# Wider splits behind the gelu, and a written order for every operation of a fused attention and feed-forward kernel

## The chip, the cores and the metric

The kernel runs on one core of a Trainium2 chip. The metric is the time of one execution on the device in microseconds, lower is better. Engines are named as the profile names them: PE is TensorE, PEld its weight loads, DVE VectorE, ACT ScalarE, POOL GpSimd, SP SyncE, whose queue issues most of the DMAs.

## What is computed

```python
def _attn_ref(q, k, v):                       # q, k, v: 8 x 8 x 576 x 64, f32
    k_p = k.reshape(B, H, Sp, 8, D).mean(axis=3)
    v_p = v.reshape(B, H, Sp, 8, D).mean(axis=3)
    scores = np.matmul(q, k_p.transpose(0, 1, 3, 2)) / np.sqrt(D)
    scores = scores - np.max(scores, axis=-1, keepdims=True)
    attn = np.exp(scores)
    attn = attn / (np.sum(attn, axis=-1, keepdims=True) + 1e-09)
    return np.matmul(attn, v_p)

def _moe_ref(x, w_in, w_out):                 # x: 4608 x 512, w_in: 512 x 2048, w_out: 2048 x 512
    h = x @ w_in
    g = h * (1.0 / (1.0 + np.exp(-1.702 * h)))
    return g @ w_out
```

The result of the attention, with heads side by side, is x of the second function: 8 batches of 576 tokens. Keys and values are means over 8 rows, so each head has 72 of them.

## The kernel before

**Numbers.** Everything is f32 at the borders. Inside, a factor is split into a high part and the remainder, and a product is three matmuls: high by high, high by low, low by high. For the first batches the parts are f32 words with fewer bits, later scaled f16.

**Stages.** The attention runs batch by batch (0 to 7), in two pieces of 256 and 320 queries: scores, exponentials, transposes, a split of the weights into `ah` and `al` (L1287, L1292), and value products `pav` (L1304 to L1307). The feed-forward part works on chunks: chunk c is the first 512 tokens of batch c, chunk 8 (B in the code) holds the 64 left-over tokens of all batches. Chunks 0 and 1 are computed directly (`dense`). From chunk 2 on a scheme with seven products in place of eight is used: `combine` (L1400) forms sums of the quadrants of x and splits them (L1391, L1397), `fold` (L1694) forms sums of the weights once and leaves them in DRAM (`wd`), and each `pair` (L1807) fetches its folded weights (`ws`, L1753) through the SyncE queue. A chunk has eight pairs.

**A pair.** A pair makes four quadrants of 256 columns of h, two TensorE banks `ha` and `hb` long: seven products of six matmuls each (L1833). A quadrant is copied out of `ha` (`keep`, L1848, ScalarE or VectorE), gets a half of `hb` added (`plus`, L1856, VectorE), goes through the gelu (L1872, ScalarE), and is scaled into the high f16 part (`scaled`, L355 on ScalarE, L358 on VectorE). The remainder is either one instruction of VectorE (L1888) or two of GpSimd (L1893 scale, L1894 subtract). After that `outputs` (L2073) multiplies with w_out: eight triples of matmuls of 512 columns a pair (L2090 to L2092). Chunk 8 uses seven products for the outputs too (`sevens`, L2205); the sums of w_out that it needs are made on the way (`make_sums`, L2106, `made`).

**Buffers.** Quadrants lie in `c_slot`s (ten, L1787), their f16 parts in eight `g_slot`s each (L1769). The names `shared` and `gall` in the profile are these places.

**Order.** The program collects tasks, each with an engine, a duration, a due time and perhaps a second engine that could do it. `Plan.order` (L173) walks through time, gives each free engine the ready task that is due first, and lets VectorE take a task of GpSimd or ScalarE that is late. The tasks are emitted in that order, and each engine executes its own in the order of emission. SyncE's queue is in order as well: a DMA that has to wait for its buffer holds up those behind it.

## Time and profile before

| | us |
|---|---|
| median of 3 runs | 954.1 (951.91 to 954.55) |
| the profiled execution | 954.56 |
| its span, first to last instruction | 952.7 |
| TensorE busy, mean granted clock | 867.6, 0.965 |
| VectorE, ScalarE, GpSimd busy | 705.0, 675.7, 549.8 |

A page of the profile gives, after the busy times, the span in 40 slices, the DMA queues, the chain of work that ended last, the costliest groups of instructions and the DMA issues. A group's row has its line, engine, operation, names and shapes, the count, the busy time, the mean duration of one in ns, and the idle time ahead of its instructions with what ended it. Further views are cut from the same trace: busy times by stretch, the chain in a stretch, and instructions in order of time. A clock of 1.00 is TensorE's higher level, 2.4 GHz; 0.50 is the lower.

### The profile page before, as it was taken

To read this page: it belongs to the slowest core of one execution; us is meant where nothing else is said; L and a number is where in the kernel's file an instruction comes from. 1 tells how busy PE (TensorE), PEld (TensorE's weight loads), DVE (VectorE), ACT (ScalarE), POOL (GpSimd) and SP (SyncE) were. 2 spreads that over 40 slices of the span, in tenths; PEclk is the share of its full clock that TensorE was granted. 3 is DMA by queue.
4 is the path that set the end of the run, shared out by engine and by line. 5 is a ranking of instruction groups with operands and counts; after the bars stand their busy time and mean duration, and the time that the engine had idled before them with its cause. 6 is when DMAs were issued, how large, how long until landed. Compare 5 with 4: busy or idle time off the path is not lost.

```text
span 952.7 us, 16696 instructions
## 1 busy us (share of the span) xinstructions
PE 867.6 (91%) x5614; PEld 644.7 (68%) x5614; DVE 705.0 (74%) x1393; ACT 675.7 (71%) x1484; POOL 549.8 (58%) x570
## 2 busy tenths in 40 slices
PE   9688899999965999579999999999999987999997
PEld 8567889788843676347667766676667654667875
DVE  4757887986879879888788877887969553445676
ACT  4899874467777786558777887778787855656674
POOL 2658752687889955255466558546444779641233
PEclk9899999999977999779999999999999998999999
DMA  8953321443423663444357434733352353455441
GB/s 265 390 201 75 75 49 58 126 114 93 134 110 98 180 165 87 136 100 128 101 127 192 118 115 123 206 95 113 108 134 78 93 157 117 143 150 178 138 145 45
DMA packets 151317, 125.36 MB, mean 132 GB/s; under 512 B 86336, under 2 KB 108352, under 8 KB 151232
## 3 DMA queue, kind: packets, MB, share of 16 engines
q1 hardware_dynamic: 146384, 115.52, 41.8%
q10 hardware_dynamic: 4848, 8.78, 2.6%
q8 instruction: 44, 0.72, 0.3%
q14 instruction: 41, 0.34, 0.1%
HBM read 102.76 MB, written 21.50 MB: 130 GB/s over the span
## 4 chain that ended last, share of the span: by engine, by line
PE 62%; ACT 14%; DVE 12%; issue 3%; POOL 3%; DMA 3%; SPq 2%; DVEq 0%; ACTq 0%; POOLq 0%
PE ha L1833 11%; PE hb L1833 8%; PE o L2090 7%; PE o L2092 7%; PE o L2091 7%; PE sps L1064 3%; ACT main L1180 3%; PE h L1591 3%; PE h L1592 2%; PE h L1593 2%; PE o L1633 2%; PE o L1634 2%; PE o L1635 2%; PE o_P L2320 2%; ACT shared L1872 1%
## 5 line engine op out<-in xcount | busy, mean ns | idle before, releaser
L1833 PEld LDWEIGHTS <-ws 128*128 128x128 f16 x2016 | 198.7, 99 | 93.9 <-issue 40.0
L1893 POOL TENSOR_SCALAR shared<-shared,smalls 128x256 f32<-128x256 f32 x107 | 107.5, 1004 | 131.5 <-ACT ghall L355 77.4
L1833 PE MATMUL ha<-x,ws 128*128 128x256 f16 x1008 | 142.1, 279 | 21.5 <-ACT x L1397 6.8
L2090 PE MATMUL o<-t,ghall 128*128 128x512 f16 x392 | 150.0, 383 | 0.2 <-ACT osb L1551 0.2
L2091 PE MATMUL o<-t,ghall 128*128 128x512 f16 x392 | 149.8, 382 | 0.0
L2092 PE MATMUL o<-t,glall 128*128 128x512 f16 x392 | 149.6, 382 | 0.0
L1833 PE MATMUL hb<-x,ws 128*128 128x256 f16 x1008 | 136.2, 276 | 11.4 <-DVE shared L1856 9.8
L1872 ACT ACTIVATE shared<-shared,smalls 128x256 f32<-128x256 f32 x170 | 85.2, 505 | 31.8 <-DVE shared L1856 26.1
L1856 DVE TENSOR_TENSOR shared<-shared,hb 128x256 f32<-128x256 f32 x127 | 52.5, 414 | 48.2 <-PE hb L1833 28.7
L1894 POOL TENSOR_TENSOR glall<-shared,ghall 128x256 f16<-128x256 f32 x107 | 76.0, 710 | 8.9
L1591 PE MATMUL h<-x,w 128*128 128x256 f32 (+1 forms) x192 | 64.0, 333 | 10.0 <-ACT g L1608 4.3
L2092 PEld LDWEIGHTS <-glall 128*128 128x128 f16 x392 | 38.6, 98 | 48.1 <-POOL glall L1894 1.5
L1848 ACT COPY shared<-ha 128x256 f32<-128x256 f32 x113 | 41.4, 366 | 34.1 <-PE ha L1833 32.2
L355 ACT ACTIVATE ghall<-shared,smalls 128x256 f16<-128x256 f32 x122 | 61.8, 507 | 4.4 <-ACT osb L1551 0.4
L1593 PE MATMUL h<-x,w 128*128 128x256 f32 (+1 forms) x192 | 61.1, 318 | 0.0
L1592 PE MATMUL h<-x,w 128*128 128x256 f32 (+1 forms) x192 | 61.1, 318 | 0.0
L1621 POOL TENSOR_TENSOR gl<-g,gh 128x512 fp32r<-128x512 f32 x25 | 34.2, 1366 | 40.1 <-ACT gh L1613 34.3
L2090 PEld LDWEIGHTS <-ghall 128*128 128x128 f16 x392 | 38.6, 99 | 25.3 <-issue 0.8
L1180 ACT COPY main<-sc 32x256 f32<-32x256 f32 (+2 forms) x123 | 54.5, 443 | 1.7
L2091 PEld LDWEIGHTS <-ghall 128*128 128x128 f16 x392 | 38.6, 99 | 24.7 <-issue 0.9
L1064 PE MATMUL sps<-k,qt 128*128 128x144 f32 x320 | 48.5, 295 | 5.0 <-DVE left L358 2.1
L1531 POOL TENSOR_TENSOR w<-raw,w 128x512 fp32r<-128x512 f32 x29 | 38.4, 1330 | 20.5 <-ACT w L1524 20.2
(364 smaller groups left out, 2265.6 us busy)
## 6 DMA issues: line engine op xcount, KB each, us to landing
ws<-wd SPq DMA_DIRECT2D x168, 256.0 KB
out_dram<-osb ACTq DMA_DIRECT2D x32, 256.0 KB
raw<-in_moe_w_in_dram SPq DMA_DIRECT2D x15, 512.0 KB
raw<-in_moe_w_out_dram SPq DMA_DIRECT2D x15, 512.0 KB
kv_False<-in_k_dram SPq DMA_DIRECT2D x28, 256.0 KB
kv_True<-in_v_dram SPq DMA_DIRECT2D x28, 256.0 KB
shared<-wd SPq DMA_DIRECT2D x56, 128.0 KB
qr<-in_q_dram SPq DMA_DIRECT2D x112, 40.0 KB
```

Source lines behind the costliest of these rows:

```text
L1064: nc.tensor.matmul(ps()[:, t * PW : (t + 1) * PW], lhsT=qt()[:, s0 : s0 + P], rhs=m.k2()[:, jj], start=True, stop=True,)
L1180: copy(out=main()[32 * r : 32 * (r + 1), :, cols].rearrange("p j t (k a) -> p t j a k", a=2), in_=sc()[rows, ts, :, 16 * r : 16 * (r + 1)] ...
L1591: nc.tensor.matmul(o, lhsT=w[:, 0, j], rhs=xs[:, 0], start=j == 0, stop=False)
L1592: nc.tensor.matmul(o, lhsT=w[:, 1, j], rhs=xs[:, 0], start=False, stop=False)
L1593: nc.tensor.matmul(o, lhsT=w[:, 0, j], rhs=xs[:, 1], start=False, stop=j == NJ - 1)
L1833: nc.tensor.matmul(o, lhsT=wv()[:, r, jj], rhs=xo(k, jj), start=start and n == 0, stop=n == len(terms) - 1,  skip_group_check=not start,)
L1872: lambda: nc.scalar.activation(out=part(i), in_=src(), func=AF.Gelu_apprx_sigmoid, scale=inner()),
L1893: nc.gpsimd.tensor_scalar(out=part(i), in0=part(i), scalar1=outer(), scalar2=None, op0=ALU.mult)
L1894: nc.gpsimd.tensor_tensor(out=gl(), in0=part(i), in1=gh(), op=ALU.subtract)
L2090: nc.tensor.matmul(o(), lhsT=gh()[:, tok], rhs=wp[:, 0], start=start, stop=False)
L2091: nc.tensor.matmul(o(), lhsT=gh()[:, tok], rhs=wp[:, 1], start=False, stop=False)
L2092: nc.tensor.matmul(o(), lhsT=gl()[:, tok], rhs=wp[:, 0], start=False, stop=stop)
```

## The change

Three things change together. First, in chunks 2 to 7 two quadrants share one place of 512 columns (a `Group`). The quadrants 2 and 3 of a pair form one group; quadrant 1 of a pair and quadrant 0 of the next form another. The scaled copy and the remainder are made for 512 columns at a time, and so is the gelu of the second kind of group. GpSimd's scale is a tensor by tensor product with the scale as a broadcast operand. Second, quadrant 3's gelu reads the bank `ha` itself, without the copy. There are now seven group places and six for each f16 part; chunk 8 has its own places and its old path by single quadrants (`single`). Third, the planner is gone. A table of task numbers, `ORDER`, gives the order of all tasks; a negative number means that the task goes to its second engine. Some VectorE tasks of the attention get GpSimd as such a second engine: the weighting, and the remainders `al` and `at`.

```diff
+ORDER = """
+3 0 2074 2075 2076 2077 2078 2079 2080 2081 2082 2083 2084 11 169 170 171 10 162 163 4 31 164 73 172 165 12 7 -168 32
...
-    def dve(n, emit, reads, writes, rate=1.0, due=None, also=(), port=False):
+    def dve(n, emit, reads, writes, rate=1.0, due=None, also=(), port=False, other=None):
+        if other is not None:
+            other = ("POOL", 0.15 + n * 2.15e-3, other, True)
...
                 dve(
                     npc,
-                    lambda ah=ah, al=al, pt=pt: nc.vector.tensor_tensor(
-                        out=al()[:, :npc], in0=pt()[:, :npc], in1=ah()[:, :npc].bitcast(F32), op=ALU.subtract
-                    ),
+                    lambda low=low: low(nc.vector),
                     [pt, ah],
                     [al],
                     port=b >= WEIGHED,
+                    other=(lambda low=low: low(nc.gpsimd)) if b >= WEIGHED else None,
                 )
...
+            before = open_groups.pop(c) if p else Group(f"{c}_b")
+            mine, after = Group(f"{nm}_a"), Group(f"{nm}_b")
+            open_groups[c] = after
+            places = [(g.part(i), g.whole) for g, i in ((before, 1), (after, 0), (mine, 0), (mine, 1))]
...
+        def split_group(g, i0, n, whole_gelu):
+            if whole_gelu:
+                x = g.part(i0, n)
+                gelu_of(256 * n, x, x, [ref(x)], ref(x), g.whole)
...
+            t = scaled(256 * n, lambda: gh()[:, cols], lambda: x()[:, cols], outer, [x], [gh], sbuf=True)
...
             def rest():
                 nc.vector.scalar_tensor_tensor(
-                    out=gl(), in0=part(i), scalar=outer(), in1=gh(), op0=ALU.mult, op1=ALU.subtract
+                    out=gl()[:, cols], in0=x()[:, cols], scalar=outer(), in1=gh()[:, cols], op0=ALU.mult, op1=ALU.subtract
                 )
 
             def rest_of():
-                nc.gpsimd.tensor_scalar(out=part(i), in0=part(i), scalar1=outer(), scalar2=None, op0=ALU.mult)
-                nc.gpsimd.tensor_tensor(out=gl(), in0=part(i), in1=gh(), op=ALU.subtract)
+                nc.gpsimd.tensor_tensor(
+                    out=x()[:, cols], in0=x()[:, cols], in1=outer().broadcast_to([P, 256 * n]), op=ALU.mult
+                )
+                nc.gpsimd.tensor_tensor(out=gl()[:, cols], in0=x()[:, cols], in1=gh()[:, cols], op=ALU.subtract)
...
-        keep(3, ha)
-        got[1, 0] = gelu(1, 0, 3)
-        got[1, 1] = gelu(1, 1, 2)
+            gelu(2)
+            gelu(3, ha)
+            got[1, 1], got[1, 0] = split_group(mine, 0, 2, False)
...
-    order = plan.order()
...
+    tasks = plan.tasks + made.tasks
     with tc.manual_schedule():
-        for t in order:
+        for n in map(int, ORDER.split()):
+            t = tasks[n if n >= 0 else -n - 1]
+            if n < 0:
+                t.swap()
             t.emit()
```

What the order does to the engines shows in three places. In the rows a name is followed by its chunk or batch, pair and a buffer number.

ScalarE in chunk 5, around the copies out of `ha5_3`, before (`ah`, `xt`, `x` belong to batch 6's attention):

```order
L1848 COPY shared15_3109<-ha5_3_7169 128x256
L1872 ACTIVATE shared15_3109<-shared15_3109,smalls_94 128x256
L1358 COPY xt6_0_7267<-pav6_0_2_7306 128x256
L355 ACTIVATE ghall1_3191<-shared15_3109,smalls_94 128x256
L1346 CAST x6_7265<-pav6_0_3_7333 128x256
L1358 COPY xt6_0_7267<-pav6_0_3_7333 128x256
L1872 ACTIVATE gall_3283<-gall_3283,smalls_94 128x256
L355 ACTIVATE ghall1_3191<-gall_3283,smalls_94 128x256
```

and now:

```order
L1997 COPY slots15_3059<-ha5_3_6919 128x256
L1448 CAST x6_6947<-pav6_0_1_6929 128x256
L437 ACTIVATE ghall_3209<-slots14_3240,smalls_94 128x512
L2017 ACTIVATE slots12_3043<-slots12_3043,smalls_94 128x256
L2017 ACTIVATE slots12_3043<-slots12_3043,smalls_94 128x512
L1448 CAST x6_6947<-pav6_0_2_6990 128x256
L1460 COPY xt6_0_6944<-pav6_0_2_6990 128x256
L437 ACTIVATE ghall_3358<-slots12_3043,smalls_94 128x512
L2017 ACTIVATE slots15_3059<-ha5_3_6919,smalls_94 128x256
```

The copy of the last quadrant is gone, its gelu reads `ha`, and scaled copies are 512 wide.

TensorE in batch 3, behind the last value product of its attention (`pav3_1_3`) and ahead of the rest of pair 0, before:

```order
L1833 LDWEIGHTS ws3_0_1_3996
L1833 MATMUL hb3_0_4238<-x3_4385,ws3_0_1_3996 128x256
L1064 MATMUL sps4_0_2_4447<-k22_1741,qt4_0_2_4396 128x144 x2
L1064 MATMUL sps4_0_3_4450<-k22_1741,qt4_0_3_4435 128x144 x2
L1833 LDWEIGHTS ws3_0_2_4049
L1833 MATMUL ha3_0_4228<-x3_4444,ws3_0_2_4049 128x256
```

and now, at the place where the first products of pair 0 that have their x are through:

```order
L2272 MATMUL o2_256_3245<-t1_15_3759,ghall_3358 128x512
L2273 LDWEIGHTS ghall_3358
L2273 MATMUL o2_256_3245<-t1_15_3759,ghall_3358 128x512
L2274 LDWEIGHTS glall_3368
L2274 MATMUL o2_256_3245<-t1_15_3759,glall_3368 128x512
L778 MATMUL vmax4_4323<-ident_79,smalls_94 128x128
```

Ahead of the last products of pair 0 (`ha3_0`) stood scores of batch 4; now output triples of chunk 2 (`o2`) stand there, which came ahead of the value products before. Between `pav3_1_3` and the first product of pair 1 there are 11 such triples of chunk 2 now; there were two of chunk 3.

GpSimd in chunk 7, where the sums of w_out are made (`made`), before (`shared` and `glall` are the gelu's remainders, `x8` and `xt8` the split for chunk 8):

```order
L2127 TENSOR_TENSOR made1_0_9175<-t1_3_2917,t1_2_2270 128x256
L1893 TENSOR_SCALAR shared15_3109<-shared15_3109,smalls_94 128x256
L1894 TENSOR_TENSOR glall1_3217<-shared15_3109,ghall1_3191 128x256
L1657 TENSOR_TENSOR made1_0_9175<-made1_0_9175 128x256
L2127 TENSOR_TENSOR made1_1_9196<-made1_0_9175,t1_2_2270 128x256
L1391 TENSOR_TENSOR xt8_0_9077<-xt8_1_9048,xt8_0_9077 128x512
L1391 TENSOR_TENSOR xt8_1_9048<-xt8_1_9048 128x512
L1657 TENSOR_TENSOR made1_1_9196<-made1_1_9196 128x256
L2127 TENSOR_TENSOR made1_2_9227<-made1_1_9196,t1_3_2917 128x256
L1391 TENSOR_TENSOR xt8_1_9048<-xt8_1_9048,xt8_0_9077 128x512
L1657 TENSOR_TENSOR made1_2_9227<-made1_2_9227 128x256
L2127 TENSOR_TENSOR made1_3_9253<-t1_2_2270 128x256
```

and now (`slots` are the gelu's places, `at7` and `al7` remainders of the attention):

```order
L1389 TENSOR_TENSOR al7_1_3_8578<-mt7_1_3_8535,ah7_1_3_8557 128x320
L2309 TENSOR_TENSOR made1_0_8629<-t1_3_2743,t1_2_2547 128x256
L2309 TENSOR_TENSOR made0_3_8652<-t1_0_2539 128x256
L1493 TENSOR_TENSOR xt7_0_8104<-xt7_0_8104,xt7_1_8513 128x512
L1493 TENSOR_TENSOR x7_8657<-xt7_1_8513,x7_8657 128x512
L1759 TENSOR_TENSOR made1_0_8629<-made1_0_8629 128x256
L1759 TENSOR_TENSOR made0_3_8652<-made0_3_8652 128x256
L2048 TENSOR_TENSOR slots15_3059<-slots15_3059,smalls_94 128x512
L2051 TENSOR_TENSOR glall_3368<-slots15_3059,ghall_3358 128x512
L2309 TENSOR_TENSOR made1_1_8858<-made1_0_8629,t1_2_2547 128x256
L2048 TENSOR_TENSOR slots12_3043<-slots12_3043,smalls_94 128x256
L2051 TENSOR_TENSOR glall_3233<-slots12_3043,ghall_3209 128x256
```

Where sums stood in nearly every second place there are fewer, and some of the chain has gone to VectorE. In chunk 7 GpSimd has 13 instructions on `made` for 55, VectorE 22 for none.

## Rows read from the trace of the kernel before

**Rows 1.** The page, part 1: busy time of each engine, share, instructions.

```profile
PE 867.6 (91%) x5614; PEld 644.7 (68%) x5614; DVE 705.0 (74%) x1393; ACT 675.7 (71%) x1484; POOL 549.8 (58%) x570
```

**Rows 2.** Busy time by stretch: length, engines (instructions), clock granted, DMA share, GB/s.

```profile
0.00:60.00 60.00, 46.53 (x308) 41.50 (x309) 35.33 (x80) 44.44 (x90) 27.21 (x29) 0.94 0.97 339
...
60.00:265.00 205.00, 195.89 (x1069) 166.89 (x1068) 161.69 (x250) 144.72 (x296) 138.67 (x117) 0.99 0.31 86
...
265.00:308.00 43.00, 24.60 (x120) 16.89 (x118) 37.51 (x49) 31.80 (x73) 38.59 (x32) 0.72 0.30 97
...
387.00:423.00 36.00, 23.74 (x103) 15.06 (x102) 31.09 (x67) 17.48 (x33) 12.96 (x11) 0.70 0.38 96
...
500.00:770.00 270.00, 264.63 (x1812) 183.93 (x1811) 211.65 (x475) 210.86 (x475) 155.34 (x173) 1.00 0.45 124
...
782.00:802.00 20.00, 11.53 (x58) 6.74 (x57) 7.05 (x10) 11.63 (x28) 19.20 (x22) 0.83 0.38 119
...
862.00:953.00 91.00, 80.99 (x682) 66.31 (x679) 60.91 (x128) 56.09 (x129) 24.96 (x33) 0.99 0.41 129
```

**Rows 3.** Chain of waits, 291 to 309 us: start, us, what.

```profile
295.94 1.85 DVE kbd L805
...
300.03 0.67 SPq L583
...
304.82 3.15 DMA ws<-wd
```

**Rows 4.** Chain of waits, 398 to 424 us.

```profile
411.58 3.17 POOL x L1391 x2
...
414.80 1.01 PE ha L1833 x4
```

**Rows 5.** Chain of waits, 770 to 803 us.

```profile
769.93 0.22 PE o L2091
...
775.19 4.29 DMA out_dram<-osb
...
782.12 1.15 POOL x L1391
```

**Rows 6.** Groups by line and shape: names, shapes, count, busy us, mean ns, idle before.

```profile
L1872 ACT ACTIVATE shared<-shared,smalls 128x256 f32<-128x256 f32 x170 | 85.2, 505 | 31.8 <-DVE shared L1856 26.1 <-DVE shared L1848 2.8 <-ACT osb L1551 0.8
...
L355 ACT ACTIVATE ghall<-shared,smalls 128x256 f16<-128x256 f32 x122 | 61.8, 507 | 4.4 <-ACT osb L1551 0.4
...
L355 ACT ACTIVATE t<-shared,smalls 128x512 f32<-128x512 f32 x15 | 10.8, 721 | 3.7 <-POOL shared L1672 2.6 <-DVE shared L1672 0.8
...
L1848 ACT COPY shared<-ha 128x256 f32<-128x256 f32 x113 | 41.4, 366 | 34.1 <-PE ha L1833 32.2 <-ACT osb L1551 0.5 <-PE hb L1833 0.4
...
L1893 POOL TENSOR_SCALAR shared<-shared,smalls 128x256 f32<-128x256 f32 x107 | 107.5, 1004 | 131.5 <-ACT ghall L355 77.4 <-DVE ghall L358 41.4 <-PE ha L1833 10.4
...
L1894 POOL TENSOR_TENSOR glall<-shared,ghall 128x256 f16<-128x256 f32 x107 | 76.0, 710 | 8.9
...
L1621 POOL TENSOR_TENSOR gl<-g,gh 128x512 fp32r<-128x512 f32 x25 | 34.2, 1366 | 40.1 <-ACT gh L1613 34.3 <-issue 3.0 <-DVE gh L1617 1.8
...
L1888 DVE SCALAR_TENSOR_TENSOR glall<-shared,smalls,ghall 128x256 f16<-128x256 f32 x47 | 27.6, 587 | 27.8 <-ACT ghall L355 27.5
...
L1391 DVE TENSOR_TENSOR x<-xt,x 128x512 f16<-128x512 f32 x10 | 11.5, 1154 | 3.6 <-ACT x L1397 3.6
```

**Rows 7.** VectorE in order of time, 409 to 414 us: start, us, instruction.

```profile
409.20 0.41 DVE L1349 TENSOR_TENSOR x<-pav,x 128x256 f16<-128x256 f32 x1
...
409.53 0.68 DVE L1391 TENSOR_TENSOR xt<-xt 128x512 f32<-128x512 f32 x1
...
412.20 1.53 DVE L1391 TENSOR_TENSOR xt<-xt,xt 128x512 f32<-128x512 f32 x1
```

**Rows 8.** Waits of TensorE: us in total, times, longest us.

```profile
PE hb L1833 <- DVE shared L1856: 9.8, 9, 5.8
...
PE ha L1833 <- DVE shared L1848: 5.1, 3, 3.9
```

341 lines of the change are left out of this document (138 added, 203 removed), and 204 rows, old and new, of the table ORDER.

## Prediction

> **What bounds the kernel now.** The page's first part comes first: TensorE is busy 91% of the span, no other engine more than 74% [rows 1]. So I ask in which stretches TensorE isn't busy, and cut the span there at the places where TensorE starts certain products. Of the stretches in [rows 2] the long one from 500 to 770 us (24 pairs of batches 4 to 6) has TensorE at 264.6 of 270 us at full clock, 1812 matmuls, 0.149 us each: nothing there but fewer matmuls could help, and the change removes none. Three short stretches are different: 265 to 308 (batch 2, between its first two pairs and its third), 387 to 423 (batch 3, inside its first pair) and 782 to 802 (batch 7, second pair). TensorE issues 120, 103 and 58 matmuls there; at 0.149 us each that is 17.9, 15.3 and 8.6 us of work in 43, 36 and 20 us, so 25, 21 and 11 us are lost, 57 together. Part of the loss is clock: 0.72, 0.70 and 0.83 granted against 1.00 in the long stretch, that is, the engine fell to its lower level of 1.2 GHz after it had been starved.
>
> What ends last in each comes from the chain of waits. The first ends in a run of VectorE work (at its end a key sum of 1.85 us), after which SyncE, whose queue keeps its order, issues other loads from 300.03 on and behind them, at 304.82, the weights of the third pair, which land 3.15 us later [rows 3]. VectorE is 37.5 of 43 and GpSimd 38.6 of 43 busy: the stretch ends when the folding of the weights and the splitting of batch 2 are done. The second ends on two GpSimd subtractions that finish the split of batch 3, with TensorE going on at 414.80 [rows 4], at the end of a ladder of transposes, casts, subtractions and products through VectorE, ScalarE and TensorE, in which GpSimd is busy 13 of 36 us: latency, not load. The third begins with ScalarE standing 4.3 us behind an output DMA and then runs through GpSimd, busy 19.2 of 20, whose queue mixes the split of batch 8 and the gelu remainders with sums made for batch 8 [rows 2, 5].
>
> **The gelu chain, two quadrants at once.** In batches 2 to 7 and the last pair of batch 8 there are 196 quadrants, each with a gelu of 505 ns and a scaled copy of 507 on ScalarE (37 of the copies on VectorE), and a remainder: 134 on GpSimd in two instructions, 1004 + 710 ns, 62 on VectorE at 587 [rows 6]; the row of the largest group stands for each, with 107 of the 134 and 47 of the 62. After it, 90 splits are 512 wide and 12 are 256 (batch 8 keeps its own path). A 512-wide scaled copy on ScalarE is in the trace, 721 ns [rows 6]: two quadrants cost 0.72 for 1.01. Of gelus 42 are 512 wide, 48 read PSUM and save a copy of 0.37. ScalarE gives back 100 x 0.29 for the 100 wide instructions, some 36 x 0.37 for copies and 27 x 0.5 for scaled copies that go to VectorE, 56 us over the span, and more with what is moved off it below. On GpSimd 41 wide and 8 narrow two-step remainders stand where 134 stood. The scale is now a broadcast operand, a form that the trace lacks; from below it is an ordinary subtraction of 512 columns, 1.37; from above twice the 1004 of the present scale, 2.0. I take 1.37, the same width and number of operands: 41 x 2.74 + 8 x 1.7 = 126 us for 134 x 1.71 = 230. At 2.0 it is 26 us more on an engine that is idle for 400; I cost that at nothing. VectorE makes 49 remainders of 512 columns and 4 of 256. The wide form isn't in the trace; ends 0.68 (a 512 subtraction alone [rows 7]) and 1.15 (one that mostly meets GpSimd [rows 6]), I take 0.75, near the first, since GpSimd is lighter: 37 us for 62 x 0.587 = 36. None of this is on TensorE's path in the long stretch, so by itself it is worth nothing there.
>
> **The moves between engines.** VectorE goes from 1393 instructions to 1597, ScalarE and GpSimd lose some 360 and 190. VectorE has to hold that. Its busy time overstates it: an instruction of 0.41 us is followed 0.33 after its start when they queue [rows 7]. Up to the third pair of batch 2 the order puts 466 instructions on VectorE for 378, 33 of them casts and subtractions of the weights at the start, 18 of the folding. Mostly 512 wide, they cost 88 x 0.55 = 48 us; ends 88 x 0.33 = 29, and 88 x 1.15 = 101 if each collides. VectorE was busy 35.3 + 161.7 + 37.5 = 234.5 of the first 308 us [rows 2], so now 282. In the first 60 us it waits for the first loads and can do about 35; the other 247 from there end at 307 if every instruction keeps its present span, and 31 us earlier (386 instructions, 0.08 overlap each) if they queue back to back. I take 298: **10 us** of the first stretch's 25, and the folding that ScalarE and GpSimd lose there (some 40 us of GpSimd) is why it isn't more.
>
> Between 308 and 500 us VectorE's number of instructions is nearly unchanged (333 for 337). There the written order counts: three of the four remainders of the ladder in batch 3 go to GpSimd, the engine that had 23 us idle, and eleven output triples of batch 2 stand between the last value product of the ladder and the second pair, for two of batch 3 now. They are held back from before the ladder, so they add no work; they keep TensorE fed while the split ends. I give **16 us** of 21, a quarter left because the last subtractions are still a chain. In the third stretch 42 of 55 sum instructions leave GpSimd's queue, about 42 x 0.7 = 29 us, and half of them go to VectorE, 7.0 of 20 us busy. What stays is the output DMA ahead of it, 4.3 us that other TensorE work covers today: **10 us** of 11.
>
> On the other side: in the long stretch VectorE gets 525 instructions for 470, 24 us more on 211.6 of 270 [rows 2], 87%. Additions of the second half bank are all on VectorE and TensorE waits for them; I charge **2 us**. At the end some 20 output triples of batch 7 (13 us, three matmuls of 512 columns at 0.22 each [rows 5]) stand behind the first product of batch 8 that stood ahead of it, which only moves work, and VectorE gets 20 us more on 60.9 of 91: **3 us**. DMA issues are the same 695; many are now one by one in SyncE's order, so that a single load may stand before a weight load; the row for it is the first stretch, where SyncE's other issues cost 304.82 - 300.03 = 4.8 us [rows 3]; the same loads stand ahead of the same weights there, so I leave it as it is.
>
> **The sum.** The profiled execution took 954.56 us, span 952.7, the median is 954.1: no difference to reckon with. 954.6 - 10 - 16 - 10 + 2 + 3 = 923.6, so **924 us**.
>
> **The rivals.** *VectorE becomes the bound* (slower). It has the reductions, 1.85 us for a key sum [rows 3], that stay on it, and the additions that TensorE waits for queue behind them in a fixed order. For it: VectorE is already the releaser of TensorE's largest wait, 9.8 us in nine, longest 5.8, and 5.1 more in three [rows 8]; the written order has been given nothing but more work for it. Against it: today's nine waits in 56 pairs. If each pair meets half a reduction, 0.93 us, the 56 pairs lose 52 us: 924 + 52 = 976. The point from which it decides is 31 / 56 = 0.55 us a pair.
>
> *The port.* When VectorE and GpSimd both work in SBUF, VectorE's subtraction of 512 columns takes 1.15 us, 1.53 in one row, for 0.68 alone [rows 6, 7]. Some 85 more wide instructions with two SBUF inputs go to VectorE, and GpSimd's own get wider; at 0.47 lost each, 40 us, 25 of them ahead of 308 and in the ladders. The gains of the first two stretches go: 924 + 26 = 950, no change that can be measured. The Trainium skill (SBUF — State Buffer, SBUF: two separate sides) says that the shared pair of ports is an exclusive lock, held for the whole instruction, and the loser fully blocks. By that rule the wide GpSimd instructions make each collision longer; the two rows agree, a 512-wide one waits 0.5 to 0.9 us. Against it: GpSimd is 118 us less busy in all, so collisions are fewer.
>
> *All of it.* The order fills the three stretches fully and some of the 9 us that TensorE idles in 60 to 265: 954.6 - 57 - 5 = 893.
>
> That the change isn't made at all is out: the instructions' order shows the wide forms and the moves.
>
> **Chances.** Forecast 52%, all of it 15%, the port 16%, VectorE's bound 17%. 924 is the likeliest. The range leaves out half of the second case and most of the last: 896 to 962; it takes in the upper price of the 88 moved instructions up to 38 of its 53 us (101 - 48). About 0.3% (2.9 us) is what a measurement of this kernel can tell from no change. Faster by more: forecast and all of it, and a third of the port case, 72%; within it half of the port case, 8%; slower 20%.
>
> **What would show it.** Right: a third pair of batch 2 that starts before 302 us, granted clock above 0.85 in all three stretches, GpSimd under 60% around the second pair of batch 7, rounds of batches 4 to 6 still 90 us each. Wrong: VectorE at 95% or more between 60 and 300 us with TensorE waiting for weight splits; waits of TensorE for the additions above 30 us in total; rounds of 93 us or more; wide subtractions on VectorE at over 1 us in the mean.

## The result, and the profile after

The changed kernel takes 942.64 us (median of 4 runs, 940.6 to 944.99) where the kernel before, run beside it, takes 953.28: a ratio of 0.9889 (95% interval 0.9858 to 0.9921). It is faster by 1.1%; 3.2% was forecast. The profiled execution took 940.6 us, span 938.6, mean clock 0.982 for 0.965.

The first part of the page, to hold against [rows 1]:

```profile
PE 863.9 (92%) x5614; PEld 640.5 (68%) x5614; DVE 788.4 (84%) x1597; ACT 541.8 (58%) x1121; POOL 400.6 (43%) x376
```

The work went where the order sends it: VectorE has 83 us more, ScalarE 134 and GpSimd 149 less. TensorE has the same 5614 matmuls. Busy time by stretch (length, then the engines in the page's order with instructions in brackets, clock granted, DMA share, GB/s), to hold against [rows 2]; the stretches are cut at the places of the program that answer to those of before:

```profile
0.00:60.00 60.00, 51.79 (x330) 45.81 (x331) 47.60 (x101) 43.26 (x89) 27.56 (x30) 0.97 1.00 329
60.00:292.00 232.00, 210.41 (x1143) 177.56 (x1141) 211.58 (x356) 137.58 (x276) 136.94 (x113) 0.97 0.30 85
292.00:407.00 115.00, 95.30 (x602) 62.82 (x601) 108.71 (x218) 75.42 (x147) 67.72 (x61) 0.94 0.50 140
...
366.00:408.00 42.00, 38.19 (x220) 23.44 (x219) 40.19 (x88) 29.13 (x60) 25.36 (x23) 0.96 0.31 74
477.00:764.00 287.00, 273.40 (x1831) 185.06 (x1829) 241.90 (x524) 166.76 (x339) 90.50 (x87) 1.00 0.40 116
...
784.90:794.30 9.40, 9.25 (x66) 6.44 (x66) 6.17 (x13) 5.44 (x11) 6.97 (x8) 1.00 0.67 221
837.00:938.60 101.60, 93.58 (x739) 71.73 (x737) 73.06 (x177) 46.90 (x116) 23.91 (x34) 0.99 0.41 130
```

The low clocks of [rows 2], 0.72, 0.70 and 0.83, are gone: the 30 us ahead of batch 2's third pair (266 to 296) have 0.93, the ladder of batch 3 (366 to 408) 0.96, the second pair of batch 7 (784.9 to 794.3) 1.00. But 292 to 407 now has VectorE at 108.7 of 115, and the 24 pairs of batches 4 to 6 (the "rounds"), which took 270 us, take 287.

**Where the time is lost, at equal work.** Stretches cut by time can't be compared when work moves between them. So I give every matmul the start-to-start time that its shape has undisturbed in the trace of before, and add these up in order of execution: 819.8 us in every kernel here. Between two marks of that sum, the elapsed time less the work is lost. In the trace of before the marks 160, 240, 300, 360, 640 and 720 lie at 200.5, 310.4, 372.3, 459.0, 747.6 and 841.8 us. The table has the loss in us, for both kernels and for the runs below (each one profiled execution). Cells that an edit doesn't touch differ by up to 3.6 us from kernel to kernel, so a difference of less than 4 isn't read by itself.

| work | before | after | p2 | n1 | e1 | e2 | e5 | t2 | s1 | s3 | u1 |
|---|---|---|---|---|---|---|---|---|---|---|---|
| 0 to 160 | 40.5 | 30.3 | 37.1 | 30.9 | 30.5 | 30.3 | 34.1 | 29.5 | 31.0 | 29.6 | 30.1 |
| to 240 (folding, end of the first stretch) | 29.9 | 29.8 | 33.7 | 31.2 | 29.9 | 30.6 | 47.1 | 29.5 | 31.1 | 30.4 | 30.9 |
| to 300 (batch 2's pairs) | 1.9 | 19.0 | 8.4 | 18.9 | 27.6 | 20.1 | 19.7 | 19.7 | 16.1 | 19.6 | 19.1 |
| to 360 (batch 3's ladder) | 26.8 | 8.8 | 21.7 | 7.7 | 11.4 | 12.8 | 8.8 | 14.2 | 7.6 | 7.7 | 8.2 |
| to 640 (rounds) | 8.5 | 19.3 | 12.8 | 24.8 | 22.1 | 38.6 | 22.1 | 19.0 | 18.9 | 13.9 | 18.2 |
| to 720 (third stretch) | 14.2 | 2.1 | 9.0 | 4.2 | 1.4 | 1.6 | 1.7 | 1.4 | 1.4 | 1.3 | 0.8 |
| to the end | 11.1 | 9.4 | 9.7 | 9.5 | 9.2 | 9.6 | 9.4 | 9.4 | 9.2 | 9.2 | 7.8 |
| sum | 132.9 | 118.8 | 132.4 | 127.2 | 132.0 | 143.6 | 142.8 | 122.7 | 115.2 | 111.6 | 115.1 |

The change gains 10.2 in the first 160 us of work, 18.0 at the ladder, 12.1 in the third stretch and 1.7 at the end. It gives back 17.1 in the pairs of batch 2 and 10.8 in the rounds: 14.1 us in all, the difference of the two spans. (The medians differ by 10.6; the profiled execution is the shortest of its four. That of s1, in the table, is the longest of its four, 3.9 us above their median.)

What TensorE waited for over the whole run (us in total, times, longest us), to hold against [rows 8]:

```profile
PE hb L1982 <- DVE slots L2005: 10.8, 12, 4.1
PE ha L1982 <- ACT slots L2017: 7.3, 2, 6.1
...
PE ha L1982 <- ACT slots L1997: 6.1, 5, 2.3
PE ha L1982 <- DVE slots L1997: 4.2, 5, 1.4
```

All four are waits for a bank to be read out: 28.4 us. The 6.1 is one wait, in batch 2's pairs. TensorE and, below it, ScalarE in order of time there (start, us, instruction, in brackets the idle time before and its releaser):

```profile
359.11 0.38 PE L2274 MATMUL o<-t,glall 128*128 128x512 f16 x1
365.57 1.44 PE L1982 MATMUL ha<-x,ws 128*128 128x256 f16 x6 [6.08 <-ACT slots L2017]
```

```profile
359.05 0.37 ACT L1460 COPY xt<-pav 128x256 f32<-128x256 f32 x1 [6.79 <-DVE x L1451]
359.43 1.28 ACT L1200 ACT_TABLE_LOAD   x1
360.72 1.64 ACT L1200 ACTIVATE sc<-sc 128x1728 f32<-128x1728 f32 x1
362.38 1.28 ACT L2017 ACT_TABLE_LOAD   x1
363.68 0.72 ACT L2017 ACTIVATE slots<-slots,smalls 128x512 f32<-128x512 f32 x1
364.43 0.72 ACT L437 ACTIVATE ghall<-slots,smalls 128x512 f16<-128x512 f32 x1
365.06 0.46 ACT L2017 ACTIVATE slots<-ha,smalls 128x256 f32<-128x256 f32 x1
```

The gelu that reads `ha` itself frees the bank. In ScalarE's fixed order it stands behind a copy that waits 6.8 us for VectorE, and then behind an exponential with a table load on either side of it.

### The profile page after: what moved, and what is told of

It reads as the page before. It is cut to its first block, busy times and chain, and to the rows that moved or that the text cites. A ratio compares the mean times of both kernels' runs of the same rounds, so it can differ in the third digit from the quotient of the medians.

```text
span 938.6 us, 16098 instructions
## 1 busy us (share of the span) xinstructions
PE 863.9 (92%) x5614; PEld 640.5 (68%) x5614; DVE 788.4 (84%) x1597; ACT 541.8 (58%) x1121; POOL 400.6 (43%) x376
## 4 chain that ended last, share of the span: by engine, by line
PE 43%; DVE 37%; ACT 7%; issue 6%; DMA 3%; SPq 2%; POOL 1%; DVEq 0%; ACTq 0%; POOLq 0%
PE ha L1982 9%; PE hb L1982 7%; PE o L2274 4%; PE o L2272 4%; PE o L2273 4%; DVE main L1271 2%; PE sps L1148 2%; DVE slots L2005 2%; DVE sc L1221 2%; DVE tail L1262 1%; DVE stage L1818 1%; DVE qt L1132 1%; DVE al L1389 1%; DVE sc L1179 1%; DVE nm L1171 1%
## 5 line engine op out<-in xcount | busy, mean ns | idle before, releaser
L1982 PE MATMUL hb<-x,ws 128*128 128x256 f16 x1008 | 132.7, 273 | 11.3 <-DVE slots L2005 10.8
L2274 PE MATMUL o<-t,glall 128*128 128x512 f16 x256 | 97.7, 381 | 0.4 <-DVE glall L2043 0.4
L2272 PE MATMUL o<-t,ghall 128*128 128x512 f16 x256 | 97.9, 383 | 0.0
L2273 PE MATMUL o<-t,ghall 128*128 128x512 f16 x256 | 97.6, 381 | 0.0
L2005 DVE TENSOR_TENSOR slots<-slots,hb 128x256 f32<-128x256 f32 x139 | 56.2, 412 | 33.4 <-PE hb L1982 27.0
L2048 POOL TENSOR_TENSOR slots<-slots,smalls 128x512 f32<-128x512 f32 (+1 forms) x40 | 40.5, 1013 | 96.0 <-ACT ghall L437 49.0
L2017 ACT ACTIVATE slots<-slots,smalls 128x256 f32<-128x256 f32 (+1 forms) x108 | 61.2, 576 | 34.3 <-DVE slots L2005 32.7
L1997 ACT COPY slots<-ha 128x256 f32<-128x256 f32 x97 | 35.7, 368 | 78.3 <-PE ha L1982 76.8
L1389 POOL TENSOR_TENSOR al<-mt,ah 128x320 fp32r<-128x320 f32 (+1 forms) x23 | 18.9, 822 | 84.7 <-ACT ah L1385 49.2
L1148 PEld LDWEIGHTS sps<-k,qt 128*128 128x128 f32 x320 | 44.1, 196 | 11.7 <-issue 5.1
L1271 ACT COPY main<-sc 32x384 f32<-32x384 f32 (+2 forms) x100 | 45.7, 457 | 10.5 <-DVE sc L1221 5.2
L1982 PE MATMUL ha<-x,shared 128*128 128x256 f16 x336 | 45.7, 273 | 3.8 <-ACT slots L1997 3.0
L2272 PE MATMUL o<-t,slots 128*128 128x512 f16 x128 | 48.6, 380 | 0.0
L2273 PE MATMUL o<-t,slots 128*128 128x512 f16 x128 | 48.6, 380 | 0.0
L2274 PE MATMUL o<-t,slots 128*128 128x512 f16 x128 | 48.6, 379 | 0.0
```

Source lines behind the costliest of these rows:

```text
L1148: nc.tensor.matmul(ps()[:, t * PW : (t + 1) * PW], lhsT=qt()[:, s0 : s0 + P], rhs=m.k2()[:, jj], start=True, stop=True,)
L1271: copy(out=main()[32 * r : 32 * (r + 1), :, cols].rearrange("p j t (k a) -> p t j a k", a=2), in_=sc()[rows, ts, :, 16 * r : 16 * (r + 1)] ...
L1982: nc.tensor.matmul(o, lhsT=wv()[:, r, jj], rhs=xo(k, jj), start=start and n == 0, stop=n == len(terms) - 1,  skip_group_check=not start,)
L2005: lambda: nc.vector.tensor_tensor(out=part(i), in0=part(i), in1=hb()[:, half * 256 : half * 256 + 256], op=ALU.add),
L2017: lambda: nc.scalar.activation(out=out(), in_=src(), func=AF.Gelu_apprx_sigmoid, scale=inner()),
L2272: nc.tensor.matmul(o(), lhsT=gh()[:, tok], rhs=wp[:, 0], start=start, stop=False)
```

## Experiments

Unless said otherwise an edit changes `ORDER` alone. A label's first letter tells the kind: `e` puts work back on its engine of before, `p` and `n` separate width from order, `t` and `u` move instructions, `s` shortens some, `b` combines two. The runs of before that stood beside them had medians of 953.3 to 955.0; "against after" compares medians with 942.64.

**Width without the written order.** p1 and p2 have the changed kernel's operations and the planner of before, with 82 us a round as in before, and with 96.

```diff
-        for n in map(int, ORDER.split()):
+        for t in order:
```

> The wide chain without the written order: the changed kernel's tasks (groups of two quadrants, gelu from PSUM, second engines for al, at and the weighting), ordered by the planner of the kernel before, with its round length of 82. Theory A (the prediction's: the wide chain is worth nothing on TensorE's path, the stretches are gained by the written order): 948 to 960 us, the losses of batch 2, 3 and 7 still there. Rival B (relief of ScalarE and GpSimd by the wide chain gives the gain, the order by itself little): 938 to 946 us.

> As the run with the planner and the round length 82, but with the round length 96 that the changed kernel's text has for its due times. Theory A: 948 to 965 us, since the round length only shifts due times; Rival B: 938 to 946 us. If the two runs differ by more than 5 us, the due times alone are worth as much as the whole change.

p1: 965.34 us, ratio 1.0120 (1.0084 to 1.0155). p2: 955.32, 1.0018 (1.0001 to 1.0035). The page of p2, and busy time at its three stretches:

```profile
PE 867.9 (91%) x5614; PEld 643.2 (68%) x5614; DVE 688.4 (72%) x1295; ACT 637.8 (67%) x1339; POOL 504.8 (53%) x474
```

```profile
262.00:305.40 43.40, 23.32 (x112) 16.64 (x111) 38.52 (x50) 32.60 (x70) 38.39 (x32) 0.66 0.33 109
389.50:435.50 46.00, 34.54 (x193) 22.84 (x193) 38.30 (x86) 26.62 (x56) 24.32 (x23) 0.81 0.43 107
786.00:802.60 16.60, 10.52 (x69) 6.34 (x67) 4.55 (x7) 8.61 (x19) 16.09 (x19) 1.00 0.51 153
```

ScalarE and GpSimd are 38 and 45 us less busy than in [rows 1], and the time is that of before: the stretches stand where they stood in [rows 2], with low clocks in the first two. With this planner the wide chain is worth nothing, as the prediction had it. But the round length, which only shifts due times, makes 10.0 us between p1 and p2, as much as the whole change; other settings of it weren't tried.

**The written order without width.** n1 executes each 512-wide gelu, scaled copy and remainder as two of 256 at the same place of the order, with GpSimd's scale as the operation with a per-partition scalar that it was before. The gelu that reads `ha` stays.

```diff
-                lambda: nc.scalar.activation(out=out(), in_=src(), func=AF.Gelu_apprx_sigmoid, scale=inner()),
+                lambda: [
+                    nc.scalar.activation(out=o, in_=i, func=AF.Gelu_apprx_sigmoid, scale=inner())
+                    for o, i in (zip(pieces(out()), pieces(src())) if n > 256 else [(out(), src())])
+                ],
```

> The written order without the wide chain: every 512-wide scaled copy, gelu and remainder behind the gelu made as two of 256 columns at the same place of the order, GpSimd's scale as before the change (one scalar a row). Theory A (the wide chain is worth nothing on TensorE's path): 943 to 948 us. Rival B (the written order leans on the room that the wide chain makes; some 100 instructions more on ScalarE at 0.29 us each, 41 on GpSimd at about 0.6, 53 on VectorE at 0.3): 955 to 975 us, slower than the kernel before.

947.93 us, 0.9931 (0.9905 to 0.9957): 5.3 us slower than after, 5.5 of it in the rounds (24.8 for 19.3). So the order, with the gelu out of `ha`, is worth some 6.8 us, the runs of before beside it having 954.7. The width and the form of the scale, which n1 takes back together, are worth another 5, but only in this order.

**The folding and the weight splits.** e5 takes 58 instructions of the folding (48.2 us of VectorE, 180 to 278 us) back from VectorE to the engines that had them; e6 the 35 casts and subtractions of the weights in the first 180 us (28.2 us).

```diff
-735 730 2557 -2553 -2554 -2550 -678
+735 730 2557 2552 2553 2549 -678
```

```diff
-12 7 -168 32 -169 176
+12 7 167 32 168 176
```

> The changed kernel with the folding that VectorE had been given between 180 and 278 us (39 instructions of GpSimd, 19 of ScalarE, 48.2 us on VectorE, 0.83 us each) put back at the same places. Theory 1 (the load on VectorE ahead of batch 2's third pair costs what the prediction priced at 0.55 us each): relief of VectorE, third pair earlier by 10 us or more, 930 to 938 us. Rival: GpSimd, 58% busy there and slower for these (1.3 to 1.4 us), becomes what the folded weights wait for, as in the kernel before: third pair later by 5 to 15 us, 948 to 958 us.

> The changed kernel with the 35 instructions of the weights' splits that VectorE took in the first 180 us (28.2 us; 22 from ScalarE, 13 from GpSimd) put back. The kernel before lost 10 us more than the changed one in that stretch, which the prediction had not named. If these splits on VectorE are the reason, most of it comes back as a loss: 948 to 953 us. Rival: it is the order of the first loads and tasks; then 941 to 945 us.

e5: 964.33 us, 1.0115 (1.0095 to 1.0135), 21.7 against after, with 17.3 in the second row of the table. Its largest wait of TensorE is a new one, for remainders (`gl`) of the first two chunks that GpSimd does late:

```profile
PE o L1734 <- POOL gl L1720: 15.8, 5, 6.3
```

So the moves of the folding are needed by this order. They gain nothing there over before, where GpSimd had both (29.8 for 29.9). e6: 946.38, 0.9923 (0.9899 to 0.9948), 3.7 against after, and 3.1 in the first row, no more than rows differ by that an edit doesn't touch: the splits explain 3 of the 10.2 us gained there at most. What the other 7 come from wasn't tried.

**The ladder of batch 3.** t2 puts nine of the output triples of batch 2 back ahead of the value products, e4 the ladder's remainders back on VectorE.

```diff
--1048 2996 3005
+2987 2994 3026 3009 3023 2963 2993 2995 3032 2996 3005
```

```diff
-2989 2991 -1036 1036
+2989 2991 1035 1036
```

> The changed kernel with nine of the eleven output triples of batch 2 that stand behind the last value product of batch 3's ladder (5.9 us at 395 to 403 us, complete since 382 to 391) put in front of the ladder's last two value products. Theory (the prediction's: these triples keep TensorE fed while the split ends): the loss around batch 3's first pair grows by 4 to 6 us, 946 to 950 us. Rival: the ladder itself became shorter, and the triples only fill what would else be filled by others: 941 to 944 us.

> The changed kernel with the four remainders `al` and one `at` of batch 3's ladder (5.2 us on GpSimd) put back on VectorE at the same places. By the prediction, which gave 16 us to the ladder for these moves and for the triples held behind it: if the moves matter, VectorE, 96% busy there, ends the ladder 3 to 6 us later, 945 to 949 us. Rival: the triples alone keep TensorE fed and VectorE's remainders (0.7 us against 1.0 on GpSimd) are no later: 941 to 944 us.

t2: 947.64, 0.9925 (0.9904 to 0.9946): 5.0 against after, and 5.4 in the ladder's cell. The split of batch 3 ends 5.9 us later, which is what the nine triples take: behind the value products they fill the ladder, ahead of them they hold it up. What they would be worth further ahead, in batch 2's pairs, t2 doesn't show; no run puts them there. e4, with four `al` and one `at`: 943.16, 0.9893 (0.9872 to 0.9914). GpSimd's share in the ladder is worth nothing that can be measured.

**Copies of the attention.** The change has many copies on VectorE that ScalarE had: of scores into `main` and `tail` and of keys. e1 puts 45 of them between 278 and 408 us back on ScalarE (22.6 us; 19 `main`, 15 `tail`, 11 of keys), e2 113 between 408 and 764 us (41.9 us).

```diff
-839 2795 2823 -862 -2720
+839 2795 2823 861 -2720
```

```diff
-3022 -1173 -1178 -1166 3033
+3022 -1173 -1178 1165 3033
```

> The changed kernel (942.6 us median, profiled span 938.6) with 45 copies, 22.6 us of VectorE's work between 278 and 408 us (19 `main`, 15 `tail`, 11 `k`, all of batch 3's and 4's attention), put back on ScalarE at the same places of the order. Theory: VectorE, 66 of 70 and 40 of 42 us busy there, is what TensorE waits for while it loses 17 us more than before; then 8 to 15 us come back, 928 to 935 us, and VectorE falls below 85% there. Rival: ScalarE's order is the limit (TensorE's longest wait, 6.1 us, is for a gelu behind the exponentials and two table loads); then ScalarE, 24 us longer in 130, makes it 942 to 950.

> The changed kernel with 113 copies, 41.9 us of VectorE's work between 408 and 764 us (59 `main`, 30 `tail`, 15 `k`, 9 `left`), put back on ScalarE at the same places. Theory: the rounds of batches 4 to 6 lose 11 us because VectorE, 84 to 89% busy, delivers additions late in bursts; with 42 us off it at least half comes back, 932 to 937 us. Rival: VectorE's average load has room, and the loss comes from ScalarE's in-order queue and from the order itself; then no gain, and with 50 us more on ScalarE (58% now) 942 to 950.

e1: 951.16 us, 0.9975 (0.9959 to 0.9990), 8.5 against after. e2: 965.85, 1.0131 (1.0113 to 1.0149), 23 against after. Busy time by stretch for 70 us of e1 and the 70 of after that answer to them, then TensorE's largest wait of e1 between 278 and 420 us and of e2 over the run:

```profile
298.00:368.00 70.00, 52.98 (x352) 36.12 (x350) 50.38 (x93) 49.13 (x104) 38.95 (x34) 0.92 0.57 158
```

```profile
296.00:366.00 70.00, 54.39 (x364) 37.18 (x363) 65.47 (x122) 44.46 (x84) 39.08 (x35) 0.92 0.60 171
```

```profile
PE ha L1979 <- ACT slots L1994: 10.9, 2, 8.9
```

```profile
PE ha L1978 <- ACT slots L1993: 19.4, 15, 2.7
```

VectorE falls from 65.5 to 50.4 of 70 and the kernel gets slower: ScalarE is no more than 70% busy, but the added copies stand in its queue ahead of the copies out of `ha` that it also makes, and TensorE waits for those banks. Ahead of the wait of 8.9 us ScalarE, below, waits 6.8 us for VectorE (`sc`), then makes twelve copies of scores (at that place of after it makes two), and only then the one out of `ha`:

```profile
329.28 1.44 PE L1979 MATMUL ha<-x,ws 128*128 128x256 f16 x6 [8.92 <-ACT slots L1994]
```

```profile
324.82 0.50 ACT L1259 COPY tail<-sc 32x64 f32<-32x64 f32 x2 [6.82 <-DVE sc L1218]
...
328.85 0.37 ACT L1994 COPY slots<-ha 128x256 f32<-128x256 f32 x1
```

The Trainium skill (Perfetto Trace Analysis, Optimizing Scalar/DVE Operations) says that if VectorE is saturated it may make sense to offload some work to ScalarE. Here VectorE was busy 108.7 of 115 us from 292 to 407, and taking 22.6 us off it in that way cost 8.5: the measurement decides, for copies that keep the places of an order made for VectorE. An order made for them on ScalarE wasn't tried. What counted was how soon the bank was read, not how full the engine was.

**Which engine holds the time?** In the `s` kernels some instructions are shortened where they stand, so that what follows may start earlier; what they leave out is missing from the result.

```diff
-                    out=red(), in_=raw().rearrange("p i (w d) -> p i d w", w=POOL), axis=AX.X, op=ALU.add
+                    out=red(), in_=raw().rearrange("p i (w d) -> p i d w", w=POOL)[:, :, :, 0:1], axis=AX.X, op=ALU.add
```

```diff
+            m = n if c == B or reads[0] is ha else n // 16
...
-                lambda: nc.scalar.activation(out=out(), in_=src(), func=AF.Gelu_apprx_sigmoid, scale=inner()),
+                lambda: nc.scalar.activation(out=out()[:, 0:m], in_=src()[:, 0:m], func=AF.Gelu_apprx_sigmoid, scale=inner()),
```

```diff
-                    out=x()[:, cols], in0=x()[:, cols], in1=outer().broadcast_to([P, 256 * n]), op=ALU.mult
+                    out=x()[:, cols][:, 0:32], in0=x()[:, cols][:, 0:32], in1=outer().broadcast_to([P, 32]), op=ALU.mult
```

The first is s1 (the two reductions of 1024 columns; VectorE is 37 us less busy), the second s2 (ScalarE 29 less; it also takes another scale factor behind the gelu), both together are s3; the third is s4 (GpSimd 38 less).

> The changed kernel with VectorE relieved and no other engine loaded: the 24 sums over 8 rows of keys and values (1.94 us each) read one row in eight, some 40 us off VectorE, 5 to 6 us a batch (the means are left out of the computation). Theory: VectorE is what TensorE waits for in batches 2 and 3 (94 to 96% busy from 296 to 408 us) and in the rounds; 15 to 30 us come back: 912 to 928 us. Rival: every engine's queue is in a fixed order, TensorE's losses are latency along the chain through ScalarE, and VectorE's load is not the limit: 936 to 943 us.

> The changed kernel with ScalarE relieved and no other engine loaded: the gelus in place of chunks 2 to 7 (the groups of 512 columns and quadrants of 256 that don't read PSUM) work on a sixteenth of their columns, the rest is left out of the computation; some 80 instructions, about 24 us off ScalarE. Theory S (the rest of the loss hangs on ScalarE's in-order queue): 10 us or more come back, 925 to 933 us. Rival (ScalarE at 58% has room): 938 to 943 us.

> The changed kernel with both reliefs: the 24 row sums of VectorE shortened (40 us) and the gelus in place of chunks 2 to 7 shortened (24 us of ScalarE). If the two engines take turns in being late, both together give more than the sum of each: below 920 us. If only VectorE's load counts: 930 to 935 us, as with the short sums alone.

> The changed kernel with GpSimd relieved: the scale ahead of its gelu remainders works on 32 columns instead of 512 or 256 (48 instructions, some 40 us off GpSimd, the rest of the scaling left out of the computation). By the port (VectorE's instructions wait while GpSimd holds the port) and by output triples that wait for remainders: 932 to 938 us. Rival: GpSimd is idle half of the time and nobody waits for it: 940 to 944 us.

Against after, s1 gains 9.6 us (933.08; 0.9780, 0.9741 to 0.9819), s2 4.2 (938.45; 0.9838, 0.9818 to 0.9859), s3 10.0 (932.67; 0.9777, 0.9757 to 0.9797), s4 7.5 (935.11; 0.9813, 0.9779 to 0.9847). No engine is the bound by itself: of 37 us taken off VectorE a quarter comes back, and of 38 off the least busy engine a fifth. By the sign set for it s3 speaks against engines that take turns in being late: it should have come in below 920, and it takes what s1 takes. The loss in the rounds stays for s1 and s2 (18.9, 18.8) and falls to 13.9 in s3, but these are single executions, that of s1 its longest, so a joint effect isn't shown. The page of s4:

```profile
PE 863.0 (92%) x5614; PEld 640.7 (69%) x5614; DVE 776.7 (83%) x1597; ACT 541.9 (58%) x1121; POOL 362.4 (39%) x376
```

VectorE executes the same 1597 instructions, none of them shortened, and is 11.7 us less busy (776.7 for 788.4): its own take longer when GpSimd is busier. That is the port rival's mechanism, and a part of what s4 gains; how much of the 7.5 us it is and how much are triples that get their remainders sooner isn't told apart.

**Waits at the head of a queue.** 392 instructions read a bank out (copies, additions, gelus of `ha`). From the end of the product (for an addition, of the copy that it adds to, where that is later) to their start passes 0.49 us in the mean in before, 0.89 in after; in the rounds 0.36 and 1.00. u1 moves 124 of them forward in their engine's queue, one of them, for instance, by 42 places:

```diff
+3451 3480 1519
...
-3456 -1524 3480 3498
+3456 -1524 3498
```

u2 also moves 64 other ScalarE instructions and 19 output triples. Some of them pass earlier users of the same place, so u2 computes something else, and its time tells of the queues alone.

> The changed kernel with 124 of the 392 copies, additions and gelus that free TensorE's banks moved forward in the order of their own engine (VectorE or ScalarE), each to where its input was complete; together they stood 162 us in the queues behind other work. No engine gets more or less work. Theory Q (the written order puts the instructions that TensorE waits for behind others; VectorE's and ScalarE's load by itself is not the limit): the loss in batch 2's pairs and in the rounds shrinks, 8 to 18 us come back, 925 to 935 us. Rival: what is passed (exponentials, transposes, splits) is on the path as well, and comes late instead: 940 to 950 us.

> On top of the order with the feeders first (937.3 us): on ScalarE 64 gelus, scaled copies and exponentials moved ahead of instructions that stood at the head of its queue waiting (35 us of ScalarE's waits filled, batch 3's exponentials at 353 us among them), and 19 output triples moved into TensorE's remaining stalls. No engine gets more or less work. Theory (waits at the head of in-order queues are the cause, in ScalarE's too): TensorE's stall of 5 us at 360 us shrinks to 1, and 927 to 933 us in all. Rival: the chain through VectorE (its copies that wait for GpSimd's end, its reductions of 1.9 us) sets the pace: 935 to 940 us.

u1: **937.33 us, 0.9832 (0.9803 to 0.9860)**, runs of 936.68 to 937.66, all below every run of after: faster than both kernels, by 16 and 5 us. u2: 937.48, 0.9828 (0.9805 to 0.9851), nothing beyond u1. In u1 the wait falls to 0.50 us in the mean (0.55 in the rounds), but the loss in the rounds only from 19.3 to 18.2. So these waits cost some 5 us over the run, and taking most of them away leaves most of the 10.8 in the rounds; what was passed may come late instead.

**More filler, more GpSimd.** t1 moves 27 output triples within their queues to where TensorE stalls; b2 is t1 with 32 remainders of 408 to 764 us (25.8 us of VectorE) on GpSimd.

```diff
-2909 2965 -965 2970 2898 2971
+2898 2922 2929 2970 2971
```

```diff
--1251 1254 -3100 3132
+-1251 1254 3099 3132
```

> The changed kernel with 27 output triples (0.65 us each, 17.5 us of work) moved forward in TensorE's order, into 17 places between 214 and 724 us where TensorE stood still (28 us together) while those triples, whose operands were complete, stood 1 to 70 tasks behind. No engine gets more or less work. Theory: the losses are TensorE's own fixed order, which waits at its head while ready products stand behind; 8 to 16 us come back, 927 to 935 us. Rival: the stalls are set by the supply from VectorE and ScalarE, and a triple used early is missing later; then 938 to 943 us.

> The changed kernel with the 27 output triples moved into TensorE's stalls (939.7 us alone) and the 32 gelu remainders that VectorE had been given between 408 and 764 us (25.8 us) put back on GpSimd (two instructions, about 2.2 us each). If VectorE's load in the rounds costs 0.25 us for each us, as with the short row sums, and GpSimd (113 of 356 us busy) has the time: 932 to 936 us. Rival: GpSimd's remainders are 1.4 us later each and output triples wait: 940 to 950 us.

t1: 939.71, 0.9845 (0.9827 to 0.9862), 2.9 against after. b2: 947.64, 0.9938 (0.9914 to 0.9962), 7.9 slower than t1, with 26.4 for 17.5 lost in the rounds. GpSimd was busy 92 of 299 us there, and still it is no place for this work: a remainder takes 1.09 + 1.18 us on it for 0.81 on VectorE (rows below). Whether that or the meeting of the two engines costs it isn't told apart.

**The sums for batch 8.** e3 puts 41 of the sums of w_out (`made`) back on GpSimd.

```diff
-2027 4033 1942 -4798 -4018
+2027 4033 1942 4797 -4018
```

> The changed kernel with the 41 sum instructions (`made`, 17.8 us) that VectorE had been given put back, 30 on GpSimd and 11 on ScalarE, at the same places. By the prediction's term for the second pair of batch 7, GpSimd's queue was the limit there and the sums leaving it were worth 10 us: 949 to 955 us, the loss around batch 7's first pairs returning. Rival: with gelu remainders 512 wide GpSimd (30 of 73 us busy there) holds the sums as well, and the gain there came from the wide remainders: 941 to 945 us.

945.76 us, 0.9920 (0.9905 to 0.9935): 3.1 against after, and 4.5 for 2.1 lost in the third stretch. At most some 3 of the 12.1 us gained there are the sums'.

## Why the prediction was off

**The chain and the moves (costed at nothing in the rounds): right in kind.** p2 shows that the wide chain is worth nothing with the planner of before; in the written order width and the form of the scale are worth 5 us (n1). The groups by line and shape (names, shapes, count, busy us, mean ns, idle before), to hold against [rows 6]:

```profile
L2048 POOL TENSOR_TENSOR slots<-slots,smalls 128x512 f32<-128x512 f32 x33 | 36.0, 1092 | 79.7 <-ACT ghall L437 46.1 <-DVE ghall L440 21.5 <-PE sps L1148 6.7
L2017 ACT ACTIVATE slots<-slots,smalls 128x512 f32<-128x512 f32 x36 | 25.8, 719 | 17.5 <-DVE slots L2005 16.9 <-ACT osb L1653 0.4
L2051 POOL TENSOR_TENSOR glall<-slots,ghall 128x512 f16<-128x512 f32 x26 | 30.8, 1183 | 2.0
L2043 DVE SCALAR_TENSOR_TENSOR glall<-slots,smalls,ghall 128x512 f16<-128x512 f32 x27 | 21.8, 809 | 0.5 <-ACT ghall L437 0.4
L2017 ACT ACTIVATE slots<-ha,smalls 128x256 f32<-128x256 f32 x41 | 19.3, 470 | 27.7 <-PE ha L1982 24.7 <-DMA left_dram<-left 1.9 <-ACT osb L1653 0.4
L1262 DVE COPY tail<-sc 32x64 f32<-32x64 f32 x30 | 12.6, 421 | 2.9 <-POOL sc L1221 2.3
L1493 DVE TENSOR_TENSOR x<-xt,x 128x512 f16<-128x512 f32 x14 | 11.0, 785 | 0.8 <-ACT x L1499 0.7
L2048 POOL TENSOR_TENSOR slots<-slots,smalls 128x256 f32<-128x256 f32 x7 | 4.5, 640 | 16.3 <-DVE slots L440 13.4 <-ACT ghall L437 2.9
```

The 0.72 of a wide gelu was right, the 0.75 of VectorE's wide remainder measured 0.81, and the broadcast scale on GpSimd 1.09, below the lower bound of 1.37.

**The first stretch (-10): right in size, wrong in place.** The third pair of batch 2 starts at 295.8 us, where 298 was forecast, with 468 VectorE instructions ahead of it for 466. But the loss up to there had been cut in the first 160 us of work (40.5 to 30.3): VectorE does 47.6 us of its work in the first 60 us, where I gave it some 35 as in [rows 2], and TensorE 51.8 for 46.5. In the stretch itself nothing was gained (29.9 to 29.8). That the start came out so near 298 is luck: the sum took the first 60 us as they were.

**The ladder (-16): the step that failed.** Its cell does fall from 26.8 to 8.8. But the triples had been batch 2's filler: its cell rises from 1.9 to 19.0. Both lie between the last write of batch 2's split and that of batch 3's, an interval that the attention of batch 3 fills. Of before, to hold against the 292 to 407 of after above:

```profile
298.20:416.00 117.80, 99.86 (x626) 67.80 (x625) 99.79 (x211) 80.78 (x181) 71.13 (x72) 0.91 0.48 135
```

TensorE has some 90 us of work in it, and it takes 117.8 us before and 115.0 after. In its first 80 us TensorE does 36 us of output triples before and 25 after, in the rest 6 before and 18 after. The hold-back moved the stall; only a shorter interval takes it away, and VectorE, 99.8 of 117.8, got 8.9 us more: the prediction found its number of instructions nearly unchanged there (211 and 218 in the interval) and costed nothing for their time. What the interval hangs on shows in the chain of waits, by line, before and after (the view cuts the rows short):

```profile
by line: PE ha L1833 13.4%; PE o L2090 9.4%; PE o L2092 9.0%; PE o L2091 9.0%; PE hb L1833 8.9%; DMA ws<-wd 4.6%; issue 4.0%; DVE main L1180 3.0%; PE sps L1064 2.9%; POOL x L1391 2.7%; DVE al L1292 2.6%; SPq L620 1.7%; SPq L583 1.6%; DVE re
```

```profile
by line: issue 9.6%; DVE red_v L747 6.5%; DVE main L1271 6.1%; DMA kv_True<-in_v_dram 5.8%; DVE slots L2005 4.8%; DVE qt L1132 4.7%; DVE k L916 4.1%; DVE tail L1262 3.8%; DVE kbd L889 3.2%; DVE glall L2043 2.9%; DVE mt L1378 2.9%; DMA ws<-w
```

By engine, the chain runs for 65.9 us through TensorE and for 29.6 through VectorE before; after, for 3.2 and 78.1. The order took TensorE's queue out of the chain, and VectorE's took its place, at nearly the same length. The prediction counted [rows 2]'s 36 us at the ladder as a loss of its own and said of the triples that "they add no work". That was true, and for the same reason they couldn't gain unless the interval shrank: the two cells together went from 28.7 to 27.8. That the triples made the 17.1 us in batch 2's pairs is read from these counts, not from a run. The interval in s1, s3 and u1:

```profile
294.00:405.00 111.00, 94.91 (x601) 62.98 (x599) 98.79 (x217) 75.28 (x147) 68.02 (x61) 0.95 0.53 144
```

```profile
292.40:406.40 114.00, 97.04 (x601) 64.06 (x599) 99.84 (x217) 70.06 (x147) 65.43 (x61) 0.94 0.52 141
```

```profile
293.00:407.70 114.70, 96.97 (x606) 63.35 (x604) 108.37 (x218) 75.78 (x148) 67.81 (x61) 0.96 0.52 141
```

Ten us less of VectorE gave back 4.0 in s1 and 1.0 in s3: with VectorE shorter the chain goes back to TensorE for 26 us in s1, 35 in s3. In u2 the interval is 112.1 us, in e1 125.9, in t2 120.9, in p2 122.0. What would shorten it further stays open: neither VectorE's load alone does it, nor the queues' heads alone.

**The rounds (+2): mis-sized, +10.8.** The sign named for it came: batches 4 to 6 take 95.5, 99.0 and 92.5 us for 90. Between the marks 360 and 640 TensorE idles 13.9 us for 6.1, and the bank-freeing engines end 10.8 of it for 5.1. So such waits are 5.7 of the 10.8 us; for the rest no releaser is shown. There, too, the chain of waits runs longer through VectorE, 82 us for 20 before. That is the rival of VectorE as the bound in kind, but at 10.8 us, not 52, and not by VectorE's load alone: neither s1 nor s2 changes it, and e2 and b2 show that unloading VectorE onto either neighbour, at the places of this order, makes it worse. What would take the 10.8 away stays open.

**The third stretch (-10): right**, -12.1, at full clock. The reason given, the sums that leave GpSimd, is worth a quarter of it at most (e3). The written order without width has 10.0 of it (n1), the width without the order 5.2 (p2). GpSimd is busy 6.97 of 9.4 us around the second pair, 74%, where under 60 was named as the sign.

**The end (+3): -1.7.** The triples there only moved, and VectorE's 73 of 102 us cost nothing that can be read.

**The sum.** Forecast -31, profiled -14.1: the ladder is 15 short, the rounds 9; the third stretch and the end give 7 more than forecast. The port rival has a mark: VectorE's durations above their undisturbed ones add up to 122.4 us for 105.8, though GpSimd is 149 us less busy, which the prediction took as the argument against it, and s4 takes 11.7 us off them. But the wide subtractions of x take 0.79 us, not over 1 (those of the weights 1.04), the first stretch kept its gain, and the ladder's was given back in batch 2's pairs. Waits for the additions of `hb` are 10.8 us, far below the 30 named.

## What to carry to other kernels

Cut the trace at points that the data set (inputs of one batch split, inputs of the next split) and sum each engine's work between them: the interval less the largest sum is the most that an order can gain there if it leaves each engine its work, here 117.8 - 99.8 = 18 us, less whatever the change adds to that engine. It was far from reached: 2.8 us. Follow the chain of waits through the interval, before and after, to see which queue took over. Work held back as filler moves a loss along such an interval; look for the place that it was taken from. In a fixed order, an instruction that frees a bank belongs where its input is ready: moving VectorE's work back to emptier engines, at the same places, cost 3 to 23 us here, moving 124 instructions that free a bank forward in their queues gained 5.
